# A weight load issued ahead of the opening barrier, and no closing barrier, in a decode kernel bound by its cache stream

## The chip, the cores and the metric

The kernel runs on one core of one Trainium2 chip. Time is device microseconds (us) of that core; a "span" is the same execution as its profile records it, from the first instruction of the program to the last. The timed value lies 1.6 to 2.0 us above the span of the same run, so spans are compared with spans and times with times.

In the profiles PE is TensorE (PEld its weight loads), DVE VectorE, ACT ScalarE, POOL GpSimd and SP SyncE; a q behind a name (SPq) marks an instruction that issues or waits. A packet is one piece of a transfer as the profile lists it. "Cast" is VectorE's first step on `x`, and the "hole" is a stretch in which the DMA engines lack work.

## The reference, cut to what matters

One decode step of attention with a cached K and V, times a gate from a small mixer MLP. Everything depends on `x` (4 rows of 448 values, 3.5 KB); nearly all bytes are the two caches.

```python
x  = A_x                                    # (4, 1, 448) bf16
xn = layernorm(x)
s  = attention(xn @ wq, k_cache, v_cache) @ wo   # caches: (4, 8, 8192, 256) bf16 each
g  = silu(mixer_and_mlp(xn, w1, w2, w3, w4))     # layernorms xn again; w3, w4 used, w1/w2 vanish at S = 1
return x + s * g
```

With a sequence of length 1 the shifted parts of the mixer are all zero, so the kernel loads only `wq`, `w3`, `w4`, `wo`, `x` and the caches: 279 MB.

## The kernel before

All large loads go through SyncE's queue, in this order. Every K load from the third on waits until TensorE has transposed the K block two heads back, because there are only two K buffers:

```python
def prog_sp(sp):
    sp.dma_start(vflat[1][:, 0:DK * HDH], A_wq...).then_inc(S["dwq"], 16)   # 3.67 MB
    sp.dma_start(vflat[0][:, 0:DK * FH], B_w3...).then_inc(S["dw3"], 16)    # 1.6 MB
    sp.dma_start(w4_sb..., B_w4...).then_inc(S["dw4"], 16)                  # 1.6 MB
    def load_k(h):
        if h >= 2:
            sp.wait_ge(S["v_k"], h - 1)      # K block h-2 has been transposed
        sp.dma_start(kn_dst(h), A_k_cache[b, g]...)                         # 4.2 MB
    ...
    load_k(0); load_k(1)
    load_wo(NLATE, HQ, "dwo")                                               # 2.75 MB
    for h in range(2, NH):
        load_k(h)
        load_v(h - 2)
    ...                                       # last V in four pieces, last of wo
    sp.wait_ge(S["v_out"], 1)
    store(sp, 0)
    take(sp, "dout", 16 * NDG)                # both stores have landed
```

`x` goes through ScalarE's queue, and VectorE's chain of small steps hangs on it: cast, layer norm, layer norm again, then TensorE's projections, then 14 warm-up matmuls, then the first K transposes.

```python
def prog_act(act):
    act.dma_start(x_sb[:, :], x2d).then_inc(S["dx"], 16)
    ...
def prog_dve(v):
    c(v.memset(q_ps[:, 0:QW], 0.0))
    v.wait_ge(S["dx"], 16)
    c(v.tensor_copy(x_f[:, :], x_sb[:, :]))   # the cast
    layernorm(x_f, xn_f, xn_b, 0, 1); layernorm(xn_f, xn2_f, xn2_b, 8, 2)
    ...
def prog_pe(pe, ...):
    ...                                       # projections, MLP
    for i in range(NWARM):                    # NWARM = 14
        pe.matmul(psv[0:PVW, 0:QW], pT[:, 0, 0:PVW], wq_sb[:, 0, 0:QW], ...)
    ...                                       # head 0: take "dk0", transpose K, ...
```

The program frame adds a barrier of all five engines ahead of these programs and another behind them. In each, four engines execute a drain that counts up a gather semaphore and then wait for a release semaphore; GpSimd waits for the four and releases them. In the opening one of the kernel before the four drains start at 0.00 to 0.32 us, GpSimd's release at 0.61, and the four see it at 0.66 to 0.67.

## Time and profile before

| what | value |
|---|---|
| timed | 655.15 us (654.53 to 656.17, 3 runs) |
| span of the profiled run | 653.10 us |
| first packet of SyncE's queue, last packet of `wo` | 1.77 us, 649.43 us |
| stream between them | 647.66 us |
| last matmul, stores issued, stores seen landed | 650.27, 651.13, 652.56 us |
| closing barrier | 652.57 to 653.10 us |

The page of the kernel before; each digit is a tenth of a slice of one fortieth of the span, and the queue line gives packets, MB and share of 16 DMA engines:

```profile
span 653.1 us, 22864 instructions
PE 552.8 (85%) x9937; PEld 473.5 (73%) x9937; DVE 276.1 (42%) x589; ACT 256.2 (39%) x364; POOL 13.5 (2%) x77
...
DMA  8999999999999999999999999999999999999996
...
q1 hardware_dynamic: 12328, 278.99, 99.3%
```

The DMA row is full from the second slice to the last but one: the stream of SyncE's queue (q1) sets the time, and TensorE at 85% follows it.

The timeline of the kernel before, first microseconds; columns are start, duration, engine, line, operation, and in brackets the idle time before it with what ended it:

```profile
0.73 0.58 ACTq L300 DMA_DIRECT2D x_sb<-in_A_x_dram  x1
0.74 0.41 SPq L192 DMA_DIRECT2D vb<-in_A_wq_dram  x1
1.21 0.41 SPq L195 DMA_DIRECT2D vb<-in_B_w_dram  x1
...
2.57 1.97 DVE L373 CAST x_f<-x_sb 4x448 f32<-4x448 bf16 x1 [1.16 <-DMA x_sb<-in_A_x_dram]
```

Both queues are held by the opening barrier until 0.7 us and are then released together. `x` has landed by 2.57, when the cast begins.

The timeline of SyncE, kernel before, 41 to 50 us, is the place where the stream is refilled for the first time (the third K load, then the first V load):

```profile
42.56 0.33 SPq L206 DMA_DIRECT2D kn<-in_A_k_cache_dram  x1
46.67 0.33 SPq L214 DMA_DIRECT2D vb<-in_A_v_cache_dram  x1
```

The windows view of the same kernel, 43 to 47 us; columns are the window, its length, busy time (and count) of PE, PEld, DVE, ACT, POOL, granted TensorE clock, DMA share, GB/s. A packet is counted where it starts, so a share over 1 can occur:

```profile
43.00:47.00 4.00, 3.96 (x68) 2.29 (x65) 1.24 (x5) 0.07 (x1) 0.19 (x1) 1.00 1.12 451
```

No hole here: 451 GB/s. The chain of waits of the kernel before, which ended last:

```profile
648.76 1.52 PE pst L689 x24
...
650.31 0.39 DVE res L528
...
650.72 0.38 DVE out_b L530
```

Behind it come the two stores and the closing barrier.

### The profile page before, as it was taken

How to read it: one execution, taken by the hardware profiler on the slowest of the kernel's cores; microseconds unless marked ns; L12 is line 12 of the kernel's file. 1: busy time of each engine (PE TensorE's matmuls, PEld its weight loads, DVE VectorE, ACT ScalarE, POOL GpSimd, SP SyncE). 2: the span in 40 equal slices, each digit the busy share in tenths (PEclk: the TensorE clock that was granted, in tenths of full speed). 3: DMA queues.
4: the chain of work that ended last, by engine and by line, in shares of the span. 5: the costliest groups of instructions: out<-in, count | busy, mean ns of one | idle time of the engine just before them, and what ended most of it. 6: DMA issues, size and time to landing. Idle time of an engine off the chain costs nothing. (4 is left out here: it accounts for less than half of the span.)

```text
span 653.1 us, 22864 instructions
## 1 busy us (share of the span) xinstructions
PE 552.8 (85%) x9937; PEld 473.5 (73%) x9937; DVE 276.1 (42%) x589; ACT 256.2 (39%) x364; POOL 13.5 (2%) x77
## 2 busy tenths in 40 slices
PE   1898997988888988888897887898788798888897
PEld 0487886986676887667787775797677688766785
DVE  7443554343344443434443443434344344443442
ACT  4153543443334443323443342444234344332340
POOL 2000000000000000000000000000000000000000
PEclk9798999888789878889987798989779987888999
DMA  8999999999999999999999999999999999999996
GB/s 362 444 421 421 443 421 446 421 444 423 444 423 444 421 446 421 446 421 446 421 443 423 442 425 442 425 442 425 438 429 438 429 438 429 434 434 434 434 424 288
DMA packets 12354, 279.13 MB, mean 427 GB/s; under 512 B 1205, under 2 KB 3257, under 8 KB 3769
## 3 DMA queue, kind: packets, MB, share of 16 engines
q1 hardware_dynamic: 12328, 278.99, 99.3%
q8 instruction: 7, 0.11, 0.1%
q10 hardware_dynamic: 16, 0.01, 0.0%
q14 instruction: 3, 0.02, 0.0%
HBM read 278.99 MB, written 0.00 MB: 427 GB/s over the span
## 5 line engine op out<-in xcount | busy, mean ns | idle before, releaser
L590 PE MATMUL pst<-ident_b,kn 128*128 128x128 bf16 x4096 | 345.8, 238 | 77.8 <-PEq L247 76.0
L297 ACT ACTIVATE kT<-pst 128x1024 bf16<-128x1024 bf16 x224 | 229.5, 1025 | 357.6 <-ACTq L247 356.7
L590 PEld LDWEIGHTS pst<-ident_b,kn 128*128 128x128 bf16 x4096 | 274.7, 108 | 83.4 <-issue 82.9
L295 DVE COPY kT<-pst 128x1024 bf16<-128x1024 bf16 x288 | 197.5, 692 | 260.9 <-DVEq L247 260.9
L602 PE MATMUL psc<-qc,kT 128*128 128x2 bf16 x4096 | 178.0, 164 | 0.8 <-issue 0.8
L602 PEld LDWEIGHTS psc<-qc,kT 128*128 128x128 bf16 x4096 | 156.7, 98 | 29.5 <-issue 29.1
L641 PE MATMUL psv<-vb,pT 128*4 128x512 bf16 x1056 | 86.3, 378 | 0.4 <-issue 0.4
L620 PE MATMUL psm<-sel,po 128*128 128x2 f32 x272 | 36.7, 257 | 0.5 <-PEq L247 0.5
L620 PEld LDWEIGHTS psm<-sel,po 128*128 128x128 f32 x272 | 34.7, 196 | 0.9 <-issue 0.9
L641 PEld LDWEIGHTS psv<-vb,pT 128*4 128x4 bf16 x1056 | 22.2, 82 | 15.4 <-issue 0.9
L454 DVE TENSOR_REDUCE rmax<-psc 128x2 f32<-128x128 f32 x32 | 9.3, 292 | 48.9 <-DVEq L247 48.9
L472 DVE COPY po<-psv 128x512 f32<-128x512 f32 x34 | 23.5, 692 | 3.0 <-DVEq L247 2.3
L459 DVE TENSOR_REDUCE gmax<-psm 2x1 f32<-2x128 f32 x32 | 8.9, 279 | 34.7 <-DVEq L247 34.7
L319 ACT ACTIVATE pT<-psc,negb 128x64 bf16<-128x64 f32 x66 | 20.6, 333 | 5.4 <-ACTq L247 5.4
L614 PEld LDWEIGHTS psm<-diag,ones_f 2*128 2x128 f32 x66 | 13.9, 260 | 6.4 <-issue 5.4
L282 POOL COPY qc<-qT 128x4 bf16<-128x4 bf16 x32 | 6.0, 188 | 583.3 <-DVEq L471 565.8
L614 PE MATMUL psm<-diag,ones_f 2*128 2x2 f32 x66 | 16.6, 319 | 1.1 <-PEq L247 0.9
L319 ACT ACTIVATION_READ_ACCUMULATOR pT<-psc,negb 128x1 f32 x66 | 13.6, 206 | 0.0
L610 PEld LDWEIGHTS psm<-ident_f,rmax 128*2 128x2 f32 x32 | 2.6, 80 | 14.0 <-issue 14.0
L538 PE MATMUL pst<-ident_b,xn_b 4*128 4x4 bf16 x14 | 0.6, 161 | 13.6 <-DVE xn_b L367 8.9
L632 PE MATMUL psm<-rowsum,ones_f 128*128 128x2 f32 x64 | 11.6, 251 | 0.0
L538 PEld LDWEIGHTS pst<-ident_b,xn_b 4*128 4x128 bf16 x14 | 0.5, 98 | 13.6 <-issue 8.9
(101 smaller groups left out, 119.3 us busy)
## 6 DMA issues: line engine op xcount, KB each, us to landing
kn<-in_A_k_cache_dram SPq DMA_DIRECT2D x32, 4096.0 KB, 25.2
vb<-in_A_v_cache_dram SPq DMA_DIRECT2D x31, 4096.0 KB, 30.5
vb<-in_A_wq_dram SPq DMA_DIRECT2D x1, 3584.0 KB, 11.3
vb<-in_B_w_dram SPq DMA_DIRECT2D x2, 1568.0 KB, 16.2
wo_sb<-in_A_wo_dram SPq DMA_DIRECT2D x1, 2688.0 KB, 43.2
kn<-in_A_v_cache_dram SPq DMA_DIRECT2D x1, 2048.0 KB, 24.9
kn<-in_A_v_cache_dram SPq DMA_DIRECT2D x1, 1024.0 KB, 26.9
kn<-in_A_v_cache_dram SPq DMA_DIRECT2D x2, 512.0 KB, 28.0
```

The source lines that it names most:

```text
L295: engine.tensor_copy(dst, src).then_inc(S["v_ev"], 1)
L297: engine.activation(dst, src, ACT.Copy).then_inc(S["a_ev"], 1)
L319: ins = act.activation(pv_p[:, :, hh], sc[:, :, hh], ACT.Exp, bias=negb[:, s, hh:hh + 1], scale=SCALE, accum_out=rowsum[:, s, hh:hh + 1])
L454: v.tensor_reduce(rmax[:, :], psc[h % 2][:, 0:NCH * REP].rearrange("p (k h) -> p h k", h=REP), AX.X, ALU.max).then_inc(S["v_rmax"], 1)
L459: v.tensor_reduce(gmax[:, :], psm[0:REP, 0:P], AX.X, ALU.max).then_inc(S["v_s"], 1)
L472: v.tensor_copy(po[:, slot], psv[:, 0:CP * DH]).then_inc(S["v_po"], 1)
L590: ins = pe.transpose(dst[:, t * P:(t + 1) * P], kn[:, h % 2, GC * j + kl, half * P:(half + 1) * P], ident_b[:, :])
L602: ins = pe.matmul(psc[h % 2][:, kk * REP:(kk + 1) * REP], kT[:, j % RING, t * P:(t + 1) * P], qc[:, h % 2, half, :], start=(half == 0), st ...
L614: pe.matmul(psm[:, P:P + REP], ones_f[0:REP, :], diag[:, :], start=True, stop=True).then_inc(S["p_m2"], 1)
L620: ins = pe.matmul(dst(dh)[:, 0:width], po[:, slot, i * DH + dh:(i + 1) * DH:NHALF], sel[:, i, 0:width], start=(i == 0), stop=(i == CP - 1))
L632: pe.matmul(psm[:, P + REP:P + 2 * REP], ones_f[:, :], rowsum[:, h % 2, :], start=True, stop=True)
L641: ins = pe.matmul(psv[o:o + CP * REP, 0:CP * DH], pT[:, h % 2, kk * REP:(kk + CP) * REP], src[:, kk:kk + CP, :].rearrange("p c d -> p (c d)"),
```

## The change

The intent is to save the fixed time at both ends. SyncE does not need the others in order to begin loading `wq`, so that load is moved ahead of SyncE's drain in the opening barrier. The closing barrier guards nothing that SyncE's own wait for both stores does not, so it is left out. Both are the author's reading of the program; the eight experiments below that have either edit returned correct results.

```diff
+def begin_ahead(nc, loads):
+    names = {i.name for i in loads}
+    blocks = nc.main_func.blocks
+    ...                                   # take the loads out of where they stand
+    first = blocks[0].instructions
+    at = next(n for n, i in enumerate(first)
+              if i.engine == mybir.EngineType.SP and isinstance(i, mybir.InstDrain))
+    blocks[0].instructions = first[:at] + list(loads) + first[at:]
+
+def drop_end_barrier(nc):
+    nc.main_func.blocks[-1].instructions = []
...
         def prog_sp(sp):
-            sp.dma_start(vflat[1][:, 0:DK * HDH], A_wq...).then_inc(S["dwq"], 16)
+            ahead.append(sp.dma_start(vflat[1][:, 0:DK * HDH], A_wq...).then_inc(S["dwq"], 16))
...
+    begin_ahead(nc, [a.ins for a in ahead])
+    drop_end_barrier(nc)
```

More of the change, by code (lines that the diff above doesn't have):

```diff
@@ L30, in sync @@
         self.eng.wait_ge(self.sem, self.n)
+def begin_ahead(nc, loads):
+    names = {i.name for i in loads}
+    blocks = nc.main_func.blocks
+    for b in blocks:
+        rest = [i for i in b.instructions if i.name not in names]
+        if len(rest) < len(b.instructions):
+            b.instructions = rest
+    first = blocks[0].instructions
[4 more added lines that the diff above has]
+    nc.main_func.blocks[-1].instructions = []
 def bass_recurrent_scan__gqa_block_cached__mixer_s_mlp__decode_kernel(
@@ L191, in prog_sp @@
         def prog_sp(sp):
-            sp.dma_start(vflat[1][:, 0:DK * HDH],
-                         A_wq.rearrange("d (t n) -> (d t) n", t=NHF).rearrange(
-                             "(p j) n -> p (j n)", j=DK)).then_inc(S["dwq"], 16)
+            ahead.append(sp.dma_start(
+                vflat[1][:, 0:DK * HDH],
+                A_wq.rearrange("d (t n) -> (d t) n", t=NHF).rearrange(
+                    "(p j) n -> p (j n)", j=DK)).then_inc(S["dwq"], 16))
             sp.dma_start(vflat[0][:, 0:DK * FH],
@@ L763, in prog_pe @@
                     finish()
+        marks, ahead = [], []
         block = es.enter_context(nc.Block())
-        marks = []
         @block.sync
```

## The prediction

> **What bounds the kernel now.** The DMA. The page's DMA row reads 9 in all slices but the first (8) and last (6); SyncE's queue has 99.3% of 16 engines' span. By packet times the first `wq` packet starts at 1.77 us, the last `wo` packet ends at 649.43, and between them no stretch over 0.3 us has fewer than 8 engines busy. So the span of 653.10 us is 1.77 us lead-in, 647.66 us stream, 3.67 us tail. PE (85%) follows the stream.
>
> **Lead-in (timeline of the first microseconds).** SyncE reaches its barrier drain first, at 0.00. GpSimd's drain holds the gather to 0.535; SyncE is released at 0.655 and issues `wq` at 0.740 (0.408 us long). The first packet starts 1.03 us after that.
>
> **Tail (chain of waits, timeline).** The last matmuls end at 650.27, two VectorE operations start at 650.31 and 650.72, the stores are issued at 651.13, SyncE sees both landed at 652.555. Then the closing barrier: SyncE's drain 652.635, GpSimd 652.668 and 652.746, three engines 652.79, SyncE 653.080 to 653.097. It is the last 0.53 us.
>
> **What the change does.**
> 1. `wq` is issued at about 0.00 instead of 0.74; its first packet starts near 1.03. `wq` alone fills the engines for over 8 us (estimate: 3.67 MB at 427 GB/s), and the next issue comes within about 0.9 us, so no hole opens: the whole stream moves left by about 0.74 us, and the tail with it.
> 2. SyncE joins the barrier later by the issue (0.41 us) and a drain. ScalarE's drain behind a DMA issue took 0.24 us at the end, so SyncE arrives between 0.45 and 0.70, against GpSimd's 0.535: the others are released 0 to 0.2 us later.
> 3. Cost: `x` (ScalarE's queue) now finds the engines filled with 28,672-byte packets of `wq`, which took 1.1 to 2.4 us each; before, three of its four packets started ahead of any of `wq`. [...] I estimate VectorE's first cast at 3.0 to 3.5 instead of 2.57, and TensorE's first K transpose at about 30.5 instead of 30.0. This is off the critical path: the third K load is issued at 42.56 while the queue has work to 46.67 (`wo` landing), a backlog of 4.1 us. It shrinks to about 2.9.
> 4. The closing barrier's 0.53 us leaves the span, which ends with SyncE's wait for the stores. [...] Timed, perhaps only 0.25 to 0.5 us returns[...].
>
> **Sum.** 0.74 + 0.53 = 1.27 us of span at most; I expect 1.2. Profiled span 651.9 us; time 655.15 - 1.2 = 653.95 us, range 653.2 to 655.0 (the runs of before spread over 1.6 us). Chances: faster by over 2% 0.003, within 2% 0.994, slower 0.003.
>
> **Right or wrong in the profile.** Right: `wq` issue at 0.0, first packet near 1.0; stream still 647.7; first cast later; third K issue ahead of the queue's end; last record SyncE's wait for the stores. Wrong: a hole in the DMA row near 43 to 47 us; a first packet still at 1.7; a longer stream.
>
> **What would make it wrong.** Stream rate changing between executions by more than 1 us; the late `x` draining the backlog; the timed interval beginning or ending elsewhere than the span.

## The result, and the profile after

Timed: 656.88 us median (655.45 to 657.18, 5 runs) against 655.07 us (654.53 to 656.17, 5 runs) of the kernel before. Ratios in this document are the mean time of one kernel's fast runs over that of the other's of the same rounds, so not quite the ratio of the medians: here 1.002, 95% interval 1.0007 to 1.0032. The change made the kernel 1.4 us slower by the means (656.54 against 655.10) and 1.8 us by the medians, where 1.2 us faster was predicted. The prediction was wrong.

The page of the changed kernel:

```profile
span 655.0 us, 22853 instructions
PE 553.4 (84%) x9937; PEld 473.7 (72%) x9937; DVE 274.4 (42%) x589; ACT 256.3 (39%) x364; POOL 13.5 (2%) x77
...
DMA  9989999999999999999999999999999999999996
GB/s 379 447 344 442 417 444 424 442 428 436 436 430 440 424 440 424 444 420 444 420 442 426 440 430 436 430 436 434 430 436 428 440 424 442 422 442 424 442 424 284
...
q1 hardware_dynamic: 12328, 278.99, 99.1%
```

The first slice is now a 9, as intended. But the third slice (33 to 49 us) has an 8 and 344 GB/s. The timeline of the changed kernel, first microseconds:

```profile
0.00 0.41 SPq L213 DMA_DIRECT2D vb<-in_A_wq_dram  x1
...
0.81 0.57 ACTq L322 DMA_DIRECT2D x_sb<-in_A_x_dram  x1
0.81 0.33 SPq L217 DMA_DIRECT2D vb<-in_B_w_dram  x1
...
6.82 0.38 DVE L395 CAST x_f<-x_sb 4x448 f32<-4x448 bf16 x1 [5.34 <-DMA x_sb<-in_A_x_dram]
```

`wq` is issued 0.74 us earlier, `x` only 0.07 us later than before. Yet VectorE gets `x` 4.25 us later. The SyncE timeline, 41 to 50 us, and then the windows view, 43 to 47 us, of the changed kernel:

```profile
45.19 0.33 SPq L228 DMA_DIRECT2D kn<-in_A_k_cache_dram  x1
49.30 0.33 SPq L236 DMA_DIRECT2D vb<-in_A_v_cache_dram  x1
```

```profile
43.00:47.00 4.00, 3.73 (x82) 2.62 (x80) 1.90 (x3) 1.12 (x2) 0.00 (x0) 1.00 0.77 262
```

The third K load is issued 2.63 us later (45.19 against 42.56), and the stream moves 262 GB/s there instead of 451. In packet times: the last `wo` packet ends at 45.64, and the first K packet starts at 46.16, which is 0.97 us after its issue. No packet of SyncE's queue moves in between (one 16,384-byte packet of an instruction queue does); the engines had run out one after another, the first at 43.9 us, the last at 45.64. The chain of waits after:

```profile
649.83 1.10 PE pst L764 x8
650.93 0.39 PE pst L721 x16
651.32 1.43 PE pst L711 x24
...
652.77 0.39 DVE res L550
...
653.19 0.38 DVE out_b L552
```

It is longer on TensorE: in this run TensorE was behind the stream at the end, while before it had waited for the last bytes. The following account compares the progress of the stream. It is worked out from packet times: for the bytes that the kernel before had moved at a given time, how much later (+) or earlier (-) another run had moved the same bytes. All runs are in it; the edits are explained below.

```
us, kernel before       8     28     44     46     64    120    400    600    649
changed kernel      -0.62  -0.57  -0.65  +2.02  +1.37  +1.98  +1.75  +1.62  +2.07
e1_no_end_barrier   +0.05  +0.13  +0.06  +0.30  +0.27  +0.22  +0.15  +0.21  +0.12
e2_early_wq_only    -0.61  -0.43  -0.56  +1.62  +1.09  +1.57  +1.42  +1.21  +1.62
e3_x_ahead_too      -0.69  -0.70  -0.69  +2.05  +1.46  +2.03  +1.85  +1.62  +2.00
e5_before_late_x    +0.20  +0.15  +0.11  +2.34  +1.65  +2.23  +2.02  +1.80  +2.31
e4_x_first_on_sp    -0.34  -0.32  -0.26  -0.42  -0.33  -0.30  -0.28  -0.22  -0.27
e6_after_short_warm -0.70  -0.53  -0.63  -0.36  -0.31  +0.02  -0.07  +0.09  +0.88
e7_before_short_w.  +0.08  -0.07  +0.03  +0.16  +0.25  +0.14  +0.02  +0.18  +0.10
e8_x_ahead_short_w. -0.65  -0.47  -0.59  -0.68  -0.64  -0.61  -0.64  -0.64  -0.77
e9_small_piece_ah.  -1.15  -0.67  -0.89  -0.91  -0.80  -0.80  -0.83  -0.86  -0.76
e10_x_first_short_w -0.36  -0.28  -0.35  +0.91  +0.27  +1.15  +0.91  +0.86  +1.28
```

The changed kernel leads by 0.65 us up to 44 us, as wished. It then loses 2.67 us in one place, at 44 to 46 us. Afterwards the figure wavers by some 0.6 us and ends where it stood, at +2.07. (The five rows that lose at 44 to 46 us all show 0.5 to 0.7 us less at 64 than at 46, and have lost it again by 120; why was not examined.) The span of the two profiled runs adds up: +2.06 us at the stream's last packet (651.49 against 649.43), +0.40 us from there to the last matmul (1.24 against 0.84), -0.52 us for the closing barrier, together +1.94 us (655.03 against 653.10; rounding).

### The profile page after: what moved, and what is told of

The parts are those of the page before. It is cut to its first block, busy times and chain, and to the rows that moved or that the text cites. A ratio compares the mean times of both kernels' runs of the same rounds, so it can differ in the third digit from the quotient of the medians.

```text
span 655.0 us, 22853 instructions
## 1 busy us (share of the span) xinstructions
PE 553.4 (84%) x9937; PEld 473.7 (72%) x9937; DVE 274.4 (42%) x589; ACT 256.3 (39%) x364; POOL 13.5 (2%) x77
```

## The experiments

Theory A: `x` falls behind the packets of `wq`, the chain that hangs on it runs late, the third K load is issued too late, and the stream runs dry. Theory B: leaving the closing barrier out costs time in what follows the kernel. Theory C: a stream that begins early runs slower as such.

Each has five timed runs (e6 six). The table has the profiled run of each, and the ratio of its timed runs to the kernel before (median before 655.07, 654.93, 654.86 and 655.24 us in the four sets; the three sets of experiments, e1 to e3 with e5, e4 with e6 to e8, and e9 with e10, ran on three different chips, so each is compared with the kernel before of its own set):

| run | timed median | ratio (95%) | span | cast of `x` ends | third K load issued | last `wo` packet / first K packet |
|---|---|---|---|---|---|---|
| before | 655.07 | | 653.10 | 4.54 | 42.56 | 46.37 / 44.63 |
| changed | 656.88 | 1.0020 (1.0007 to 1.0032) | 655.03 | 7.20 | 45.19 | 45.64 / 46.16 |
| e1 | 654.80 | 0.9997 (0.9983 to 1.0011) | 652.95 | 4.53 | 43.27 | 46.36 / 44.67 |
| e2 | 657.11 | 1.0027 (1.0014 to 1.0041) | 655.23 | 7.05 | 44.68 | 45.80 / 45.65 |
| e3 | 654.74 | 0.9998 (0.9984 to 1.0012) | 654.25 | 5.18 | 45.05 | 45.88 / 46.04 |
| e5 | 658.51 | 1.0055 (1.0041 to 1.0068) | 655.41 | 7.97 | 45.30 | 46.51 / 46.27 |
| e4 | 654.15 | 0.9994 (0.9981 to 1.0007) | 652.31 | 2.13 | 41.87 | 46.09 / 44.30 |
| e6 | 655.27 | 1.0007 (0.9994 to 1.0020) | 653.93 | 7.37 | 42.67 | 45.85 / 43.85 |
| e7 | 655.33 | 1.0005 (0.9992 to 1.0018) | 653.88 | 4.54 | 43.11 | 46.30 / 44.52 |
| e8 | 654.42 | 0.9989 (0.9976 to 1.0002) | 652.57 | 5.24 | 41.44 | 45.66 / 43.98 |
| e9 | 654.22 | 0.9984 (0.9970 to 0.9997) | 652.29 | 4.60 | 42.15 | 45.53 / 43.74 |
| e10 | 655.46 | 1.0003 (0.9989 to 1.0016) | 654.65 | 2.13 | 44.02 | 45.99 / 44.97 |

In the last column a K packet that starts before the last `wo` packet ends means that the engines pass from one load to the next one by one, which alone does not exclude a hole: some engines may have run out before (e2, e5, e10). Counted from packet times, the 16 engines lacked packets of SyncE's queue between 42 and 49 us for 2.05 us on average in the changed kernel, 1.60 in e2, 2.01 in e3, 1.40 in e5 and 0.58 in e10, and for at most 0.07 us in the other seven.

### e1: only the closing barrier left out

```diff
-    begin_ahead(nc, [a.ins for a in ahead])
     drop_end_barrier(nc)
```

> Only the closing barrier is left out; the opening is as before. Theory A (the late x makes the loss): VectorE's first cast at 2.6 us and third K issue at 42.6 as before, no idle time of the stream at 44 to 48 us, span about 652.6, timed about 0.25 to 0.5 us faster than before. Theory B (leaving the closing barrier out is what costs, in what follows the kernel): timed 1 us or more slower than before. Theory C (a stream that begins early runs slower as such): as A here.

The stream was that of the kernel before (it ends at 649.41 against 649.43), and nothing became slower, so theory B falls. The gain was smaller than expected. The closing barrier's 0.52 us was gone from the trace, but in this run TensorE's last matmul came 1.25 us after the stream's end instead of 0.84, so the span was only 0.15 us shorter. The third K load, untouched by this edit, went out at 43.27, so this point scatters by 0.7 us of itself; 43.27 + 0.97 is still ahead of the first K packet at 44.67. Timed, the difference is unclear (medians 654.80 and 654.93; one run of the kernel before in this set took 658.47 and widens the intervals of e1, e2, e3 and e5). So how much of the 0.5 us reaches the timed value stays unsettled: TensorE's place behind the end of the stream scatters by as much (0.77 to 1.68 us over the profiles).

### e2: only the early load

```diff
     begin_ahead(nc, [a.ins for a in ahead])
-    drop_end_barrier(nc)
```

> Only wq goes ahead; the closing barrier stays. Theory A: like the changed kernel and 0.5 us longer: cast at 6 to 7 us, third K issue near 45, about 2 us of idle stream at 44 to 48, span about 655.5, timed about 2 us slower than before. Theory B: about 0.7 us faster than before. Theory C: slower as in A, and the loss is spread over the stream, not in the hole.

It was slower, as theory A and theory C expected, and the loss was at 44 to 46 us (from -0.56 to +1.62) and not spread over the stream. This speaks against theory C.

### e5: the kernel before, with `x` alone a little later

```diff
         def prog_act(act):
+            act.wait_ge(S["g_c"], 2)
             act.dma_start(x_sb[:, :], x2d).then_inc(S["dx"], 16)
```

> The kernel before, with ScalarE waiting for GpSimd's first two memsets (about 0.4 us later) before it issues x; wq and both barriers untouched. Theory A: x now falls behind wq's packets, lands 3 to 5 us later, third K issue about 2.5 us later, near 45, against a queue that still lasts to 46.7: a hole of about 1 us or less, span 653.3 to 654.5. Theory B and theory C: span as before within 0.4 us, since the stream begins as before.

Nothing but the issue of `x` was touched: `wq` was issued at 0.74 and both barriers were in place. Timeline of this run:

```profile
0.74 0.41 SPq L192 DMA_DIRECT2D vb<-in_A_wq_dram  x1
1.11 0.57 ACTq L301 DMA_DIRECT2D x_sb<-in_A_x_dram  x1
...
7.59 0.38 DVE L374 CAST x_f<-x_sb 4x448 f32<-4x448 bf16 x1 [6.18 <-DMA x_sb<-in_A_x_dram]
```

and its windows view at 43 to 47 us:

```profile
43.00:47.00 4.00, 3.81 (x81) 2.69 (x79) 2.03 (x3) 1.29 (x2) 0.00 (x0) 1.00 0.99 331
```

Issuing 3.5 KB 0.38 us later made the cast begin 5.0 us later and cost 3.6 us by the medians, more than the changed kernel lost and more than expected (the hole took 2.2 us of the profiled run, which was the fastest of its five; what made the other four 0.9 to 1.6 us slower than it has no profile and stays open). A late `x` alone, without the change, opens the hole, and theories B and C cannot explain that.

### e3: `x` ahead of the barrier as well

```diff
-            act.dma_start(x_sb[:, :], x2d).then_inc(S["dx"], 16)
+            ahead.append(act.dma_start(x_sb[:, :], x2d).then_inc(S["dx"], 16))
```
(each load is placed ahead of its own engine's drain)

> The changed kernel, with the load of x put ahead of ScalarE's part of the opening barrier as well. Theory A: x finds at most one packet of wq ahead of it on its engines, cast before 4 us, third K issue at or before 43, no hole, span about 651.8 to 652.2, timed about 1 us faster than before. Theory B and theory C: still about 1.5 to 2 us slower than before.

This was a half miss. `x` was issued at 0.115 us; its packets started at 2.7 to 3.3 us, behind 0.46 to 0.80 MB of `wq` instead of 1.46 to 1.66 MB, and the timed loss was gone (ratio 0.9998). But no gain was left, and the profiled run, the slowest of the five, still had the hole. ScalarE's issue and drain delayed the whole barrier to 1.03 us, the warm-ups took 5.1 us instead of 4.5 (5.0 in the changed kernel), and TensorE stood 1.67 us within the first head, near the end of its transposes. Such a stall is in five of the twelve profiles (0.84 us in the kernel before and in e1, 0.27 in the changed one, 0.20 in e5; none in e6). In all five it ends 1.3 to 1.5 us after a 16,384-byte packet of the profile's instruction queue q8 has ended; what TensorE waits for there was not tested. It lies ahead of the third K load's release, so it probably has a part in e3's hole.

### e4: `x` first in SyncE's own queue, then `wq`, both ahead

```diff
-            act.dma_start(x_sb[:, :], x2d).then_inc(S["dx"], 16)
...
         def prog_sp(sp):
+            ahead.append(sp.dma_start(x_sb[:, :], x2d).then_inc(S["dx"], 16))
             ahead.append(sp.dma_start(vflat[1][:, 0:DK * HDH], A_wq...
```

> The changed kernel, but SyncE issues x, then wq, both ahead of its part of the opening barrier; so x is first in the same queue, and ScalarE issues nothing at the start. Theory A: x lands near 2.5 us or earlier, first cast ends at 4.6 us or earlier as in the kernel before, wq's first packet between 1.3 and 1.6, third K issue near 42.6 to 43.4, no hole, span 652.0 to 652.6, timed 0.5 to 1 us faster than before. Rival (an early stream of wq is itself the loss): slower than before, as in the changed kernel.

As theory A expected: the packets of `x` started at 0.94 to 0.99 us and the first packet of `wq` at 1.40, the third K load went out at 41.87, the hole was gone, the stream's lead of 0.3 us lasted to its end, and the span was 652.31. Timed, the gain is within the noise. Theory C needs an early stream to be slow; here it is not. The cast took 0.37 us, from 1.76 to 2.13, before GpSimd's large memsets (from 3.05). In the kernel before it took 1.97 us and ended at 4.54, just after GpSimd's last memset ended at 4.29; in e1, e7 and e9, whose casts also began during these memsets (2.40 to 3.58), it took 1.55, 2.13 and 1.02 us and ended at 4.53 to 4.60 as well. Why it is longer during the memsets was not tested. It matters for the account: the kernel before already lost 1.6 us in that cast, so the 4.25 us by which `x` came late in the changed kernel became only 2.66 us at the end of the cast.

### e6 and e7: fewer warm-up matmuls, after and before

```diff
-    NWARM = 14
+    NWARM = 6
```

> The changed kernel with 6 warm-up matmuls instead of 14 ahead of the first K transposes: x stays late. Theory A (the late x costs only because TensorE then frees the first K buffer too late): K transposes start about 2.9 us earlier than in the changed kernel, third K issue near 42.3, hole at 44 to 48 us gone, span about 652, timed about 1 us faster than before, 2.5 us faster than the changed kernel. Rival (the loss is not that hole): time as the changed kernel.

> The kernel before with 6 warm-up matmuls instead of 14, as a control for the run above. Theory A: the stream has no hole there to close, so the third K load is issued 1.5 us or more earlier and the span stays within 0.4 us of 653.0. Rival (the warm-ups are on the critical path anyway): faster by about 2 us, as in the run above.

In e6 `x` was as late as in the changed kernel, but the third K load went out at 42.67 and the hole was closed; windows view, 43 to 47 us:

```profile
43.00:47.00 4.00, 3.95 (x70) 2.29 (x68) 1.24 (x5) 0.00 (x0) 0.18 (x1) 1.00 1.20 468
```

So in the profile the late `x` costs the stream nothing up to 64 us once that refill is in time. The timed runs do not show this as clearly: e6 was 1.0 us faster than the changed kernel (mean times 655.53 and 656.54, from different sets, with overlapping intervals of their ratios), not 2.5. Its profiled run kept the lead of 0.3 to 0.7 us to 64 us, lost it by 120 us and lost 0.7 us more within the last microsecond of the stream; spans of its six runs lie in two groups, 652.6 to 652.9 and 653.9 to 655.2. What makes the second group is open.

The control e7 missed its number in an instructive way. The stream was unchanged, as expected, and the time not clearly different (the span, 653.88, missed the 0.4 us allowed, because TensorE ended 1.68 us after the stream), but the third K load was issued 0.55 us later, not 1.5 us earlier. TensorE timeline of e7, and then of e6, at the first K transposes:

```profile
25.55 2.77 PE L582 MATMUL psv<-vb,pT 128*32 128x512 bf16 x6
29.59 1.86 PE L590 MATMUL pst<-ident_b,kn 128*128 128x128 bf16 x16 [1.27 <-PEq L247]
```

```profile
28.42 2.64 PE L604 MATMUL psv<-vb,pT 128*32 128x512 bf16 x6
30.99 1.07 PE L612 MATMUL pst<-ident_b,kn 128*128 128x128 bf16 x16
```

In e7 the warm-ups ended before the first K block had landed (29.46 us), TensorE stood idle for 1.27 us, and its first 16 transposes took 1.86 us. In e6, with late `x`, there was no idle time, and they took 1.07 us. The granted clock was 0.50 from 29.6 to 31.5 us in e7 and 1.00 from 31.0 to 32.1 us in e6, and the two durations differ by a factor of 1.7. What sets the granted clock was not tested. The 14 warm-ups bridge the wait for K in the kernel before: they ran from 25.57 to 30.09 us, K landed at 29.47, and the 16 transposes took 1.07 us at a granted clock of 1.00. With a late `x` they stand in the way: in the changed kernel K landed at 29.62, but the warm-ups ran from 28.26 to 33.30, and the first transpose came at 33.23.

### e8: `x` ahead and 6 warm-ups

```diff
-    NWARM = 14
+    NWARM = 6
-            act.dma_start(x_sb[:, :], x2d).then_inc(S["dx"], 16)
+            ahead.append(act.dma_start(x_sb[:, :], x2d).then_inc(S["dx"], 16))
```

> The changed kernel with x ahead of ScalarE's part of the barrier and 6 warm-up matmuls. Theory A: slack on both sides, third K issue before 43.5 [...], no hole, span 651.8 to 652.2 in every run and less scatter than with x ahead alone; timed about 1 us faster than before. If a hole is left, something other than x and the warm-ups holds the first head.

The third K load went out at 41.44, there was no hole, and the stream kept the whole 0.65 us lead to its end. The spans of the five runs were 651.9 to 652.9, a narrower band than e3's 652.1 to 654.2, but not as low as expected, because TensorE ended 1.61 us after the stream in the profiled run. Timed it gained 0.65 us by the means, which is just within the noise (the interval's upper end is 1.0002).

### e9: only a small first piece of `wq` ahead

```diff
-            ahead.append(sp.dma_start(vflat[1][:, 0:DK * HDH], A_wq...))
+            ahead.append(sp.dma_start(vflat[1][:, 0:HDH], wq_src[:, 0:HDH]).then_inc(S["dwq"], 16))
+            sp.dma_start(vflat[1][:, HDH:DK * HDH], wq_src[:, HDH:DK * HDH]).then_inc(S["dwq"], 16)
...
-            take(pe, "dwq", 16)
+            take(pe, "dwq", 32)
```

> The changed kernel, with wq cut in two: only its first seventh (4,096-byte packets, eight an engine) goes ahead of the barrier, the rest follows it; x is issued as in the changed kernel. If x waits for packets that the engines were already given (three an engine in the changed kernel, 28,672 bytes each), the same number of small ones costs it about 0.5 us: its packets start before 2.8 us, the first cast ends by 4.7 us, third K issue near 43, no hole, the stream stays ahead of the kernel before by 0.3 to 0.7 us, span about 652.3. If x falls behind the large packets of the second part as well, its packets start at 4 us or later and the hole of 1 to 2 us is back.

Timeline of e9 at the start:

```profile
0.00 0.41 SPq L215 DMA_DIRECT2D vb<-in_A_wq_dram  x1
...
0.81 0.57 ACTq L324 DMA_DIRECT2D x_sb<-in_A_x_dram  x1
0.81 0.33 SPq L217 DMA_DIRECT2D vb<-in_A_wq_dram  x1
...
3.58 1.02 DVE L397 CAST x_f<-x_sb 4x448 f32<-4x448 bf16 x1 [2.10 <-DMA x_sb<-in_A_x_dram]
```

SyncE at 41 to 50 us, and windows view at 43 to 47 us:

```profile
42.15 0.33 SPq L230 DMA_DIRECT2D kn<-in_A_k_cache_dram  x1
46.25 0.33 SPq L238 DMA_DIRECT2D vb<-in_A_v_cache_dram  x1
```

```profile
43.00:47.00 4.00, 3.95 (x68) 2.52 (x65) 1.47 (x5) 0.49 (x1) 0.19 (x1) 1.00 1.19 483
```

The issue times of `wq` and `x` are those of the changed kernel to a hundredth of a microsecond. What was issued ahead of `x` differs: 0.52 MB in packets of 4,096 bytes instead of 3.67 MB in packets of 28,672. `x`'s packets started at 2.78 to 3.04 us (a little later than the 2.8 expected) instead of 5.07 to 5.30, the cast ended at 4.60, the hole was gone, and the stream led by 0.8 us to its end. This version beats both kernels: 654.22 us median, ratio 0.9984 to the kernel before with an interval that excludes 1, about 1.05 us by the means (654.16 against 655.21). It is close to what the change was predicted to give. But the reckoning in the expectation, three packets an engine, did not hold: 123 to 139 packets (7.7 to 8.7 an engine), nearly all of the small ones and 3 to 11 of the next part's, started ahead of those of `x`. The run does not separate the size of the packets from the amount issued ahead.

### e10: `x` first on SyncE and 6 warm-ups

```diff
-    NWARM = 14
+    NWARM = 6
-            act.dma_start(x_sb[:, :], x2d).then_inc(S["dx"], 16)
...
+            ahead.append(sp.dma_start(x_sb[:, :], x2d).then_inc(S["dx"], 16))
```

> x, then wq, on SyncE ahead of the barrier, with 6 warm-up matmuls instead of 14, closing barrier left out: no cause is tested here, but whether this is the best of the set. The stream leads the kernel before by 0.3 us as with 14 warm-ups, no hole, third K issue before 42; span 651.9 to 652.7, the tail of TensorE deciding within that; timed 0.5 to 1 us faster than before.

A miss. `x` was early, so the short warm-ups left TensorE idle for 3.56 us before the first K block landed; its first 16 transposes took 1.87 us (1.07 in the kernel before), the third K load went out at 44.02, and the stream lost 1.26 us at 44 to 46. This is the same hole, now made by TensorE's slow start and not by `x`.

## Why the prediction was wrong, point by point

- **The bound.** Right: the stream of SyncE's queue sets the time. "The tail follows the stream" was only half right: in the changed kernel and in e1, e2 and e6 to e10, TensorE's last matmuls ended 1.24 to 1.68 us after the stream, against 0.77 to 0.84 us where it waited for the last bytes. That is scatter of up to 0.9 us that the early load does not cause (e1 shows it with the opening untouched, e7 with both barriers in place).
- **Step 1, the early load.** Right: issue at 0.00, first packet at 1.02 us (predicted near 1.03), and the stream led by 0.65 us (predicted 0.74) up to 44 us.
- **Step 2, the barrier.** Right: the others were released 0.07 us later (predicted 0 to 0.2); SyncE's drain behind the issue took 0.12 us.
- **Step 3, the cost of a late `x`.** This is the step that failed, in two terms. First, "I estimate VectorE's first cast at 3.0 to 3.5" was 6.82, and the first K transpose came at 33.2 us instead of about 30.5. I had reckoned that `x` would wait for one packet of `wq` an engine; that was my estimate, which no trace on record then showed. By packet times 1.46 to 1.66 MB of `wq` had been started ahead of `x`'s four packets, which is 51 to 58 of the 28,672-byte packets, or 3.2 to 3.6 on each of 16 engines (3.2 to 3.4 in e5, 1.0 to 1.75 in e3); e9, with a smaller amount in smaller packets ahead, got `x` in 2.3 us sooner from the same issue time. What decides how much is let past first was not tested. Second, "a backlog of 4.1 us. It shrinks to about 2.9": the time to the landing of `wo` is not the slack. The third K load took 0.97 us from issue to its first packet in the changed kernel (0.95 to 0.99 in e2, e3, e5 and e10), and the first engine was out of `wo` at 44.63 in the kernel before, well before the landing was seen at 46.67. So the real slack was 44.63 - 42.56 - 0.97 = 1.1 us. Against it stood 2.63 us of later issue and 0.73 us of an earlier end of the queue: 3.36 - 1.1 = 2.3 us was to be lost, and 2.67 us was measured, restart included (the engines' first K packets started at 46.16 to 47.05).
- **Step 4, the closing barrier.** The 0.52 us left the span as predicted. What of it reaches the timed value was not resolved (e1).
- **Signs named in advance.** "Wrong: a hole in the DMA row near 43 to 47 us" was the sign that appeared, and "the late `x` draining the backlog" was listed among what could make the prediction wrong. The mechanism had been seen; its size was taken from the wrong unit, and its limit from the wrong pair of events.

## What to carry to other kernels

When a large load is moved ahead, ask which small load on another queue it now overtakes, and what hangs on that one; here 3.5 KB decided over 4 MB. Two ways of keeping the early start worked here: the small load first in the same queue (e4), or only a small first piece of the large one, in small packets, ahead (e9). Here the slack of the queue, counted from when the refill's first packet could start to the moment the first engine ran out, was 1.1 us; counted from its issue to the landing of `wo` it had seemed 4.1. Such slack is worth computing before anything is moved upstream of it.
